# Attention followed by a two-level mixture of experts: earlier query loads, a split first load, regrouped gates, rare cases out of line

## The chip, the core and the metric

The kernel runs on one core of a Trainium2 chip. The metric is the device time of one execution in microseconds (us); before the change it is 521.31 us, the median of 3 runs (520.46 to 521.45). The profile that is read below is one further execution of the same kernel, with a span of 519.0 us.

The engines are named as the profile names them: PE is TensorE (matmuls), PEld its weight loads, DVE is VectorE, ACT is ScalarE, POOL is GpSimd, SP is SyncE, which here only starts transfers. A trailing q (ACTq, SPq) is the engine's instruction queue: waits, branches, register loads and the starting of transfers.

## The reference

Eight batches of attention with 16 query heads and one shared key/value head, then a mixture of experts in which a token goes to one group of four and to one expert of four in that group.

```python
# q: (8,16,384,64)   k, v: (8,1,384,64)   w1: (4,4,1024,1024)   w2: (4,4,1024,1024), all float32
scores = (q @ k^T) / 8
attn   = softmax(scores)                 # minus the row maximum, over 384 keys
x      = (attn @ v), heads joined        # (3072, 1024)
g_idx  = argmax(x @ w_group);  g_w = softmax(x @ w_group)[g_idx]
e_idx  = argmax(x @ w_expert[g_idx]);  e_w = softmax(...)[e_idx]
out    = g_w * e_w * (relu(x @ w1[g_idx, e_idx]) @ w2[g_idx, e_idx])
```

## The kernel before

**Tiling.** A batch's 16 heads times 384 queries are cut into six chunks of 2 x 512 query columns; two chunks make a *pair* `p`, so a batch has three pairs (`r` = 0, 1, 2) and the whole has 24. For every chunk `g` and each of three key tiles `kt`, `scores(g, kt)` (line 187) makes 128 x 1024 scores in one of two PSUM tiles `s` and ACT exponentiates them into `pt` (line 193). No row maximum is taken off. `values(g)` (line 247) multiplies `pt` by the values into the PSUM tile `o`, of which there is one. DVE sums the three exponent tiles (`pre_add`), and the column sums come either from a PE matmul (`sum_keys`, line 221, PSUM `kss`, turned by DVE into `krow`) or from a DVE transpose and reduction (`fold_keys`). `invert` (line 232) brings the sums to a PSUM tile `sm`, DVE takes the reciprocal `rc` and spreads it to `rinv`; `weigh` (line 256) multiplies `o` by it into `xT`, the layer's input for that batch, of which there is one buffer.

**Experts.** For each batch the gate has three steps: `gate_a` (line 269, PE: the sixteen-plus-four logits in partial sums `gps`, copied by ACT to `part`), `gate_b` (line 279, PE: `lps`; then `gate_math` on DVE and ACT), and `gate_c` (line 317, PE: counts `cps`; then the most frequent expert is found on DVE and GpSimd starts the 4 MB of that expert's weights). The whole batch is pushed through that expert; tokens of another expert are dealt with at the end, and with the given inputs at most one such (batch, expert) pair is left. The expert's work is cut into 14 units per batch (8 of `hps`, line 351, and 6 of `yps`, line 360) and `fill(n)` emits n of them. ACT takes `hps` and `yps` out of PSUM and SP stores `y`.

**Order.** Nothing is scheduled by the compiler: each engine's instructions run in the order in which this Python program emits them. The loop over pairs (line 407) has two forms. For `p` below `MOE_AT` = 7 (the *attention pairs*) no expert work exists yet, the column sums come from `sum_keys`, and the gates stand at the end of a pair: `gate_a` and `gate_b` of batch `b - 1` at the end of the pair with `r` = 0 (so in pairs 3 and 6), `gate_c` at the end of the pair with `r` = 1 (pairs 4 and 7). From pair 7 on (the *mixed pairs*) `fill` puts expert units between the parts of attention, and `gate_b` is emitted in pieces between the matmuls of a unit. At pair 7 that is done for batch 1, for which pair 6 has already done it.

**Loads.** `load_q(p)` (line 73) brings a pair's 512 KB of queries in four transfers of 128-byte runs; the tile `qraw` has three buffers, and the last reader of a buffer is `stats_q` (line 159), an ACT pass that sums squares. Both stand at the very end of a pair: `stats_q(p)`, then `load_q(p + 3)`. `prep_q(p + 1)` (line 177) is a DVE transpose of `qraw` into `qT` near the head of pair `p`. The keys and values of the next batch are started on ACT's queue (`load_kv`, line 81) at the end of a pair with `r` = 0. All transfers from SP and ACT share eight completion semaphores; a transfer waits until the one eight places before it has landed.

**Head and tail.** The kernel begins with 30 + 12 matmuls on ones (`warm`, lines 100 and 386), which compute nothing, while SP starts the first keys and then the first queries. At the end one more expert is applied to up to 128 collected tokens and scattered to the output (line 640); then every engine loads three flags into registers (lines 642 to 644), runs a loop over further (batch, expert) leftovers, here zero times (line 650), and a branch around a full recomputation for inputs whose scores are too large for the exponential without a maximum, here not taken (line 654).

Of the kernel before, what the change touches and what calls it, by code (L numbers as in the profile page):

```python
# [21 lines left out]
def kernel(  # L22
# [50 lines left out]
    def load_q(p):  # L73
        b, r = divmod(p, NCH // 2)
        t = pool.tile([P, NBP, 32], FP32, tag="qraw", bufs=3, name="qraw")
        for a in range(2):
            for j in range(2):
                nc.sync.dma_start(out=t[64 * a + 32 * j:64 * a + 32 * j + 32], in_=qv[b, a, j, :, r * NBP:(r + 1) * NBP])  # L78
        q_raw[p] = t

    def load_kv(b):
        kt = pool.tile([P, NB, 32], FP32, tag="k", name="k")
        for a in range(2):
            for j in range(2):
                (nc.sync if b == 0 else nc.scalar).dma_start(out=kt[64 * a + 32 * j:64 * a + 32 * j + 32], in_=kv[b, 0, j])
        k_raw[b] = kt
        vt = pool.tile([P, ST, D], FP32, tag="v", name="v")
        nc.scalar.dma_start(out=vt[:], in_=v[b, 0].rearrange("(st p) d -> p st d", st=ST))
        v_sb[b] = vt
# [12 lines left out]
    make_identity(nc, ident)  # L102
    load_kv(0)
    load_q(0)
# [164 lines left out]
    def gate_a(b):  # L269
        ps = ps_o.tile([P, CW], FP32, tag="o", name="gps")  # L270
        for r in range(2):
            for j in range(4):
                ko = 4 * r + j
                nc.tensor.matmul(out=ps[32 * j:32 * j + 32, 0:S], lhsT=gw[:, ko, :], rhs=xT[b][:, ko * S:(ko + 1) * S], start=(r == 0), stop=(r == 1), tile_position=(0, 32 * j))  # L274
        t = pool.tile([P, S], FP32, tag="part", bufs=1, name="part")
        nc.scalar.copy(out=t[:], in_=ps[:, 0:S])
        part[b] = t

    def gate_b(b, between=False):
        ps = (ps_m if between else ps_o).tile([P, ST, 32], FP32, tag="mm" if between else "o", name="lps")  # L280

        def logits(st):
            nc.tensor.matmul(out=ps[:, st, :], lhsT=part[b][:, st * P:(st + 1) * P], rhs=sel[:], start=True, stop=True)  # L283
        if between:
            for st in range(ST):
                inserts.append((0, lambda st=st: logits(st)))
            inserts.append((0, lambda: gate_math(b, ps)))
        else:
            for st in range(ST):
                logits(st)  # L290
            gate_math(b, ps)
# [25 lines left out]
    def gate_c(b):  # L317
        ps = ps_o.tile([P, ST, GE], FP32, tag="o", name="cps")
# [66 lines left out]
    for _ in range(12):  # L385
# [21 lines left out]
    for p in range(NP + 1):  # L407
# [3 lines left out]
        if p < NP:  # L411
            scores(g, 0)
            scores(g, 1)
            pre_add(g, 1)
# [6 lines left out]
        if p > 0:  # L421
            values(g - 2)
            if p - 1 < MOE_AT:
                sum_keys(p - 1)
# [3 lines left out]
        if p < NP:  # L428
            scores(g, 2)
            scores(g + 1, 0)  # L430
        if p > 0:
            if not busy:
                values(g - 1)
# [26 lines left out]
        if not busy:  # L460
            if r == 2 and b + 1 < B:
                stats_k(b + 1)
            if r == 0 and 0 < b < B:
                gate_a(b - 1)
                gate_b(b - 1)
            if r == 1 and b > 0:
                gate_c(b - 1)
            fold_last()
        elif p < NP:
# [7 lines left out]
            if r == 0 and 0 < b < B:  # L477
# [5 lines left out]
        if p < NP:  # L483
            stats_q(p)
            if p + 3 < NP:
                load_q(p + 3)
# [134 lines left out]
    nc.vector.tensor_copy(out=oki[:], in_=okf[:])  # L621

# [19 lines left out]
    ok = nc.values_load(oki[0:1, 0:1], min_val=0, max_val=1, skip_runtime_bounds_check_because="the result of a comparison")  # L642
    n_done = nc.values_load(nex[0:1, 0:1], min_val=0, max_val=1, skip_runtime_bounds_check_because="the result of a comparison")
    n_extra = nc.values_load(nex[0:1, 1:2], min_val=0, max_val=NPAIR, skip_runtime_bounds_check_because="a sum of 128 flags")

# [4 lines left out]
    with tc.For_i(n_done, n_extra, 1) as i:  # L650
# [3 lines left out]
    with tc.If(ok < 1):  # L654
        x_dram = nc.dram_tensor("x_t", [B * H, D, S], FP32).ap()
        qf = q.rearrange("b h (st p) d -> (b h) p st d", st=ST)
        kf = k.rearrange("b o (st p) d -> (b o) p st d", st=ST)
        vf = v.rearrange("b o (st p) d -> (b o) p st d", st=ST)
        with tc.For_i(0, B * H, 1) as i:
            bk = nc.s_assert_within(i >> 4, 0, B - 1, skip_runtime_bounds_check_because="the bits of an index below 128")  # L660
            qs = pool.tile([P, 4, ST, D], FP32, tag="qraw", bufs=3, name="qs")
            nc.sync.dma_start(out=qs[:, 0], in_=qf[bass.ds(i, 1)].rearrange("a p st d -> (a p) st d"))
            nc.sync.dma_start(out=qs[:, 1], in_=kf[bass.ds(bk, 1)].rearrange("a p st d -> (a p) st d"))
            vs = pool.tile([P, ST, D], FP32, tag="v", name="vs")
            nc.sync.dma_start(out=vs[:], in_=vf[bass.ds(bk, 1)].rearrange("a p st d -> (a p) st d"))
            qk = pool.tile([D, 2, S], FP32, tag="pt", bufs=8, name="qk")
            for a in range(2):
                tp = ps_m.tile([P, CW], FP32, tag="mm", name="tp")
                for st in range(ST):
                    nc.tensor.transpose(out=tp[0:D, st * P:(st + 1) * P], in_=qs[:, a, st, :], identity=ident[:])  # L670
                nc.vector.tensor_copy(out=qk[:, a, :], in_=tp[0:D, 0:S])
            ot = pool.tile([D, S], FP32, tag="rinv", bufs=1, name="ot")
            for qt in range(ST):
                sp = ps_s.tile([P, 2, CW], FP32, tag="s", name="sp")
                nc.tensor.matmul(out=sp[:, 0, 0:S], lhsT=qk[:, 0, qt * P:(qt + 1) * P], rhs=qk[:, 1, :], start=True, stop=True)
                sm1 = pool.tile([P, 4], FP32, tag="sm1", bufs=2, name="sm1")
                nc.vector.reduce_max(out=sm1[:, 0:1], in_=sp[:, 0, 0:S], axis=AX)
                nc.vector.tensor_scalar(out=sm1[:, 1:2], in0=sm1[:, 0:1], scalar1=-scale, scalar2=None, op0=OP.mult)
                at = pool.tile([P, S], FP32, tag="presum", bufs=3, name="at")
                nc.scalar.activation(out=at[:], in_=sp[:, 0, 0:S], func=ACTF.Exp, bias=sm1[:, 1:2], scale=scale)  # L680
                nc.vector.reduce_sum(out=sm1[:, 2:3], in_=at[:], axis=AX)
                nc.vector.reciprocal(out=sm1[:, 3:4], in_=sm1[:, 2:3])
                nc.vector.tensor_scalar(out=at[:], in0=at[:], scalar1=sm1[:, 3:4], scalar2=None, op0=OP.mult)
                tp = ps_m.tile([P, CW], FP32, tag="mm", name="tp")
                for kt in range(ST):
                    nc.tensor.transpose(out=tp[:, kt * P:(kt + 1) * P], in_=at[:, kt * P:(kt + 1) * P], identity=ident[:])
                av = pool.tile([P, S], FP32, tag="pt", bufs=8, name="av")
                nc.vector.tensor_copy(out=av[:], in_=tp[:, 0:S])
                op = ps_o.tile([P, CW], FP32, tag="o", name="op")
                for kt in range(ST):  # L690
                    nc.tensor.matmul(out=op[0:D, 0:P], lhsT=vs[:, kt, :], rhs=av[:, kt * P:(kt + 1) * P], start=(kt == 0), stop=(kt == ST - 1))
                nc.vector.tensor_copy(out=ot[:, qt * P:(qt + 1) * P], in_=op[0:D, 0:P])
            nc.sync.dma_start(out=x_dram[bass.ds(i, 1)].rearrange("a d s -> (a d) s"), in_=ot[:])
        xr = x_dram.rearrange("(b a hp) d s -> b a d hp s", b=B, a=2)
        zero = pool.tile([P, Dm], FP32, tag="pt", bufs=8, name="zero")
        nc.vector.memset(zero[:], 0.0)
        for b in range(B):
            xT[b] = pool.tile([P, KO * S], FP32, tag="xT", bufs=1, name="xT")
            for a in range(2):
                nc.sync.dma_start(out=xT[b][a * D:(a + 1) * D].rearrange("p (hp s) -> p hp s", hp=KO), in_=xr[b, a])  # L700
            xg = pool.tile([P, KO * S], BF16, tag="xbf", bufs=4, name="xg")
            nc.vector.tensor_copy(out=xg[:], in_=xT[b][:])
            nc.sync.dma_start(out=xb_dram[b], in_=xg[:])
            gate_a(b)
            gate_b(b)
            for st in range(ST):
                nc.sync.dma_start(out=outv[b, :, st, :], in_=zero[:])
        with tc.For_i(0, NPAIR, 1) as i:
            add_pair(i)
# [31 lines left out]
```

## Time and profile before

| | us |
|---|---|
| time, median of 3 | 521.31 |
| span of the profiled execution | 519.0 |
| start of the first scores matmul | 9.53 |
| starts of pairs 2, 3, 4, 5, 6, 7, 8 (first scores matmul) | 30.66, 43.99, 61.04, 75.22, 88.40, 105.51, 126.72 |
| end of the last ACT instruction (`yc`) | 508.7 |
| scatter started by GpSimd | 509.0 |

The starts of the pairs come from the timeline, which lists instructions in order of time, merged when alike and adjacent: start, duration, engine, line, operation, output and inputs, shapes, count, and in square brackets the idle time of the engine before it with what ended that idle time. The view of waits lists, for each engine and line, whom it waited for: total us, how often, the longest. PE's own waits are few, since it is busy nearly throughout, so the list of them is short and can be read as a whole.

### The profile page before, as it was taken

To read this page: it belongs to the slowest core of one execution; us is meant where nothing else is said; L and a number is where in the kernel's file an instruction comes from. 1 tells how busy PE (TensorE), PEld (TensorE's weight loads), DVE (VectorE), ACT (ScalarE), POOL (GpSimd) and SP (SyncE) were. 2 spreads that over 40 slices of the span, in tenths; PEclk is the share of its full clock that TensorE was granted. 3 is DMA by queue.
4 is the path that set the end of the run, shared out by engine and by line. 5 is a ranking of instruction groups with operands and counts; after the bars stand their busy time and mean duration, and the time that the engine had idled before them with its cause. 6 is when DMAs were issued, how large, how long until landed. Compare 5 with 4: busy or idle time off the path is not lost.

```text
span 519.0 us, 6961 instructions
## 1 busy us (share of the span) xinstructions
PE 487.0 (94%) x2605; PEld 205.8 (40%) x2605; DVE 342.8 (66%) x485; ACT 240.4 (46%) x342; POOL 63.7 (12%) x64
## 2 busy tenths in 40 slices
PE   6999889989999999999999999999989999998991
PEld 4233323334433444344433444344433444454550
DVE  3687577769948798779945995969856984322000
ACT  2645374426453645545635545454644742322331
POOL 1011113102101011101100030101110210210000
PEclk8999999999999999999999999999999999999996
DMA  9472249961995379754986299646963296699980
GB/s 127 45 83 42 72 63 177 208 134 15 201 201 178 60 122 216 175 119 78 212 136 199 48 170 204 180 79 118 214 110 127 56 201 130 185 232 248 226 224 14
DMA packets 148377, 73.06 MB, mean 141 GB/s; under 512 B 122587, under 2 KB 122587, under 8 KB 148336
## 3 DMA queue, kind: packets, MB, share of 16 engines
q0 software_dynamic: 19008, 37.84, 40.3%
q1 hardware_dynamic: 114928, 32.53, 30.2%
q10 hardware_dynamic: 14400, 2.16, 2.3%
q8 instruction: 23, 0.38, 0.3%
q14 instruction: 18, 0.15, 0.1%
HBM read 91.31 MB, written 19.40 MB: 213 GB/s over the span
## 4 chain that ended last, share of the span: by engine, by line
PE 61%; DMA 17%; SPq 7%; ACT 5%; DVE 5%; issue 3%; ACTq 1%; POOL 0%; POOLq 0%; DVEq 0%
PE s L191 17%; DMA qraw<-in_q_dram 14%; PE o L254 14%; PE yps L360 13%; PE hps L351 12%; SPq L78 7%; PE gps L274 2%; ACT pt L193 2%; DMA out_dram<-y 2%; DVE qT L182 2%; ACT junk L161 1%; PE kss L226 1%; ACT y L362 1%; DMA k<-in_k_dram 1%; PE lps L283 1%
## 5 line engine op out<-in xcount | busy, mean ns | idle before, releaser
L193 ACT ACTIVATE pt<-s 128x1024 f32<-128x1024 f32 x144 | 139.4, 1019 | 123.2 <-PE s L191 123.2
L191 PE MATMUL s<-qT,kT 64*128 64x512 f32 x576 | 145.1, 622 | 5.3 <-DVE qT L182 3.5
L254 PE MATMUL o<-pt,v 128*64 128x512 f32 x576 | 130.4, 598 | 0.0
L360 PE MATMUL yps<-w,hT 128*128 128x512 bf16 x384 | 90.0, 379 | 5.4 <-DVE rc L240 4.2
L351 PE MATMUL hps<-xbf,w 128*128 128x384 bf16 x512 | 89.2, 326 | 2.3 <-ACT hT L353 0.9
L201 DVE TENSOR_TENSOR presum<-pt 128x1024 f32<-128x1024 f32 x48 | 61.1, 1272 | 37.0 <-ACT pt L193 37.0
L263 POOL CAST xbf<-xT 128x1024 bf16<-128x1024 f32 x24 | 40.7, 1696 | 341.2 <-DVE xT L262 341.2
L191 PEld LDWEIGHTS s<-qT,kT 64*128 64x128 f32 x576 | 49.6, 188 | 64.8 <-issue 43.4
L254 PEld LDWEIGHTS o<-pt,v 128*64 128x64 f32 x576 | 38.6, 136 | 87.8 <-issue 74.9
L351 PEld LDWEIGHTS <-w 128*128 128x128 bf16 x512 | 48.7, 99 | 44.1 <-issue 14.5
L205 DVE TENSOR_TENSOR presum<-presum,pt 128x1024 f32<-128x1024 f32 x48 | 58.6, 1220 | 2.7 <-ACT hT L353 0.5
L362 ACT ACTIVATE y<-yps,gsel 128x512 f32<-128x512 f32 x48 | 32.9, 686 | 59.2 <-PE yps L360 55.2
L360 PEld LDWEIGHTS <-hT 128*128 128x128 bf16 x384 | 37.1, 101 | 56.7 <-issue 19.4
L182 DVE STREAM_TRANSPOSE qT<-qraw 128x1024 f32<-128x1024 f32 (+1 forms) x25 | 29.8, 1196 | 30.9 <-DMA qraw<-in_q_dram 24.8
L353 ACT ACTIVATE hT<-hps 128x384 bf16<-128x384 f32 x64 | 31.2, 490 | 39.6 <-PE hps L351 37.1
L213 DVE STREAM_TRANSPOSE turn<-presum 128x1024 f32<-128x1024 f32 x34 | 42.4, 1246 | 1.2
L217 DVE TENSOR_REDUCE fold<-turn 128x32 f32<-128x1024 f32 x34 | 41.5, 1220 | 1.2
L161 ACT ACTIVATE junk<-qraw 128x1024 bf16<-128x1024 f32 x24 | 25.2, 1052 | 15.3 <-DMA k<-in_k_dram 15.2
L242 DVE STREAM_TRANSPOSE rinv<-rc 128x1024 f32<-128x1024 f32 x24 | 29.9, 1245 | 0.8
L262 DVE TENSOR_TENSOR xT<-o,rinv 128x1024 f32<-128x1024 f32 x24 | 29.4, 1225 | 1.3
L240 DVE RECIPROCAL rc<-sm 128x32 f32<-128x32 f32 x24 | 8.0, 335 | 24.7 <-PE sm L236 15.4
L93 POOL DMA_DIRECT2D w<-in_moe_w_dram x18 | 12.6, 704 | 61.0 <-DVE gsel L339 42.4
(130 smaller groups left out, 179.9 us busy)
## 6 DMA issues: line engine op xcount, KB each, us to landing
w<-in_moe_w_dram POOLq DMA_DIRECT2D x18, 1024.0 KB, 13.4
w<-in_moe_w_dram POOLq DMA_DIRECT2D x9, 2048.0 KB, 24.3
qraw<-in_q_dram SPq DMA_DIRECT2D x96, 128.0 KB, 3.8
out_dram<-y SPq DMA_DIRECT2D x48, 256.0 KB, 3.7
x_bf<-xbf SPq DMA_DIRECT2D x8, 768.0 KB, 3.3
k<-in_k_dram ACTq DMA_DIRECT2D x28, 48.0 KB, 2.3
v<-in_v_dram ACTq DMA_DIRECT2D x8, 96.0 KB, 2.6
xe<-x_bf SPq DMA_DIRECT2D x1, 768.0 KB, 9.7
```

The source lines that it names most:

```text
L182: nc.vector.transpose(out=t[:, i * w:(i + 1) * w], in_=src[:, i * w:(i + 1) * w])
L191: nc.tensor.matmul(out=ps[:, par, :], lhsT=kT[b][r, kt * P:(kt + 1) * P], rhs=qT[g][r, :], start=True, stop=True)
L193: nc.scalar.activation(out=t[:], in_=ps[:], func=ACTF.Exp, scale=scale)
L201: nc.vector.tensor_add(out=t[:], in0=pt[g, 0][:], in1=pt[g, 1][:])
L205: nc.vector.tensor_add(out=t[:], in0=t[:], in1=pt[g, 2][:])
L213: nc.vector.transpose(out=t[:], in_=presum[g][:].rearrange("p a n -> p (a n)"))
L217: nc.vector.reduce_sum(out=fold[p][:, ch, :], in_=t[:].rearrange("p (b i) -> p b i", i=32), axis=AX)
L254: nc.tensor.matmul(out=o_ps[p][64 * par:64 * par + 64, ch, :], lhsT=v_sb[b][:, kt, :], rhs=pt[g, kt][:, par, :], start=(kt == 0), stop=(kt ...
L263: nc.gpsimd.tensor_copy(out=xbf[b][:, cs], in_=xT[b][:, cs])
L351: nc.tensor.matmul(out=ps[:, 0:S], lhsT=w1[:, ko, fc * P:(fc + 1) * P], rhs=xb[:, ko * S:(ko + 1) * S], start=(ko == 0), stop=(ko == KO - 1))
L360: nc.tensor.matmul(out=ps[:], lhsT=state["h"][:, fo, st * P:(st + 1) * P], rhs=w2[:, fo, nh * CW:(nh + 1) * CW], start=(fo == 0), stop=(fo ...
L362: nc.scalar.activation(out=y, in_=ps[:], func=ACTF.Copy, scale=gs[:, st:st + 1])
```

## The change

The change has five parts.

1. **Query loads at the head.** `stats_q(p)` and `load_q(p + 3)` move from the end of pair `p` to just after its first two `scores`.
2. **First loads over two queues.** The first query tile is loaded in two halves by SP, ahead of everything else; the first keys go to ACT's queue and the first values to SP's. The second group of warm-up matmuls grows from 12 to 36. `values(0)` is emitted in pair 0 instead of pair 1.
3. **First gates over two pairs.** For batches 0 and 1, `gate_a` moves from the end of pairs 3 and 6 to just after the first two `scores` of pairs 4 and 7; `gate_b` of batch 0 to the middle of pair 4, before `values`; batch 1 keeps only the `gate_b` of pair 7; `gate_c` of batch 0 moves behind `fold_last`. These use the PSUM pair `mm` in place of the single tile `o`. The last batch's `gate_b` uses `mm` too.
4. **`sum_keys`** of the attention pairs moves from before to after the middle two `scores`.
5. **Rare cases out of line.** One flag, "anything rare to do", is worked out from the two existing ones and loaded into a register of every engine before the last expert units; the loop and the recomputation, with their own register loads, stand inside one branch that is placed out of line.

```diff
-    def load_q(p):
+    def load_q(p, parts=1):
...
-                nc.sync.dma_start(out=t[64 * a + 32 * j:64 * a + 32 * j + 32], in_=qv[b, a, j, :, r * NBP:(r + 1) * NBP])
+        n = NBP // parts
+        for i in range(parts):
...
-                (nc.sync if b == 0 else nc.scalar).dma_start(out=kt[64 * a + 32 * j:64 * a + 32 * j + 32], in_=kv[b, 0, j])
+                nc.scalar.dma_start(out=kt[64 * a + 32 * j:64 * a + 32 * j + 32], in_=kv[b, 0, j])
-        nc.scalar.dma_start(out=vt[:], in_=v[b, 0].rearrange("(st p) d -> p st d", st=ST))
+        (nc.sync if b == 0 else nc.scalar).dma_start(out=vt[:], in_=v[b, 0].rearrange("(st p) d -> p st d", st=ST))
...
+    load_q(0, 2)
     load_kv(0)
-    load_q(0)
...
     prep_k(0)
-    for _ in range(12):
+    for _ in range(36):
         nc.tensor.matmul(out=warm[:, 0:P], lhsT=ones_bf[:], rhs=ones_bf[:], start=True, stop=True)
...
             scores(g, 0)
             scores(g, 1)
+            stats_q(p)
+            if p + 3 < NP:
+                load_q(p + 3)
+            if r == 1 and 1 < p <= MOE_AT:
+                gate_a(b - 1, True)
             pre_add(g, 1)
...
-            values(g - 2)
-            if p - 1 < MOE_AT:
+            if p > 1:
+                values(g - 2)
+            if busy and p - 1 < MOE_AT:
                 sum_keys(p - 1)
...
             scores(g + 1, 0)
+        if p == 0:
+            values(0)
         if p > 0:
             if not busy:
+                sum_keys(p - 1)
+                if r == 1 and 0 < b < B:
+                    gate_b(b - 1)
                 values(g - 1)
                 invert(p - 1)
...
-            if r == 0 and 0 < b < B:
-                gate_a(b - 1)
-                gate_b(b - 1)
+            fold_last()
             if r == 1 and b > 0:
-                gate_c(b - 1)
-            fold_last()
+                gate_c(b - 1, True)
...
-            if r == 0 and 0 < b < B:
+            if r == 0 and MOE_AT <= p - r and 0 < b < B:
                 gate_a(b - 1)
...
-        if p < NP:
-            stats_q(p)
-            if p + 3 < NP:
-                load_q(p + 3)
...
+    nc.vector.tensor_tensor(out=raref[:, 0:1], in0=small[0:1, 1:2], in1=small[0:1, 0:1], op=OP.is_gt)
+    nc.vector.tensor_scalar(out=raref[:, 1:2], in0=okf[:], scalar1=-1.0, scalar2=1.0, op0=OP.mult, op1=OP.add)
+    nc.vector.tensor_add(out=raref[:, 0:1], in0=raref[:, 0:1], in1=raref[:, 1:2])
...
+    nc.vector.tensor_copy(out=rarei[:], in_=raref[:, 0:1])
+    rare = nc.values_load(rarei[0:1, 0:1], min_val=0, max_val=2, skip_runtime_bounds_check_because="a sum of two comparisons")
...
-    with tc.For_i(n_done, n_extra, 1) as i:
+    rare_block = tc.If(rare > 0, preferred_fallthrough_block=False)
+    with rare_block:
...
+      with tc.For_i(n_done, n_extra, 1) as i:
         add_pair(pair_of(ids[0:1, bass.ds(i, 1)]))
```

## The prediction

> **What bounds the kernel now.** I read the page's busy line first, then PE's own waits, then the timeline where those waits lie. PE is busy 94% of the span; no other engine is above 66%:
>
> ```profile
> PE 487.0 (94%) x2605; PEld 205.8 (40%) x2605; DVE 342.8 (66%) x485; ACT 240.4 (46%) x342; POOL 63.7 (12%) x64
> ```
>
> So the time is PE's work plus its gaps. The gaps are 519.0 - 487.0 = 32 us: about 1.4 before the first matmul, 11 after the last (PE's last matmuls end at 508), and some 20 in PE's waits, the largest of which are:
>
> ```profile
> PE yps L360 <- DVE rc L240: 4.2, 4, 1.6
> PE s L191 <- DVE qT L182: 3.5, 1, 3.5
> PE sm L236 <- DVE krow L228: 1.4, 1, 1.4
> PE lps L283 <- ACT part L276: 1.2, 2, 0.6
> PE gps L274 <- DVE xT L262: 1.2, 1, 1.2
> PE cps L319 <- DVE xT L262: 1.2, 1, 1.2
> PE gps L274 <- issue: 1.1, 1, 1.1
> ```
>
> The reader should see three families: the head (`s` waits for `qT`), the gates in the attention pairs (`gps`, `lps`, `cps`, `sm`), and four waits in the mixed pairs. The timeline around one of these four shows its cause:
>
> ```profile
> 267.29 1.25 DVE L182 STREAM_TRANSPOSE qT<-qraw 128x1024 f32<-128x1024 f32 x1 [6.07 <-DMA qraw<-in_q_dram]
> ...
> 268.46 0.32 DVE L240 RECIPROCAL rc<-sm 128x32 f32<-128x32 f32 x1
> 268.82 1.25 DVE L242 STREAM_TRANSPOSE rinv<-rc 128x1024 f32<-128x1024 f32 x1
> 268.83 1.45 PE L360 MATMUL yps<-w,hT 128*128 128x512 bf16 x6 [1.20 <-DVE rc L240]
> ```
>
> Queries land late, DVE waits 6.07 us for them, `rc` stands behind that transpose on DVE, and the PSUM buffer that `rc` must read is the one the next `yps` needs. At the end, the branch around the recomputation (line 654) is what the span waits for:
>
> ```profile
> L654 PEldq COMPARE_BRANCH  x1: 3762/3762/3762, 514.2 to 514.2; - x1
> ```
>
> PE takes 3.76 us for it, after the scatter has landed (SP and ACT leave line 650's waits at 513.4).
>
> [...] the granted clock is 0.50 from about 9.45 to 12.9, 3.4 us, after PE stood idle from 6.01 to 9.53. Before 9.45 the record shows 1.00, but the 30 first warm-up matmuls took 3.38 us, 0.113 each, against 0.061 for the same size in line 632 (32 in 1.95), so I take that stretch as half rate too. [...] each start takes 0.4 to 0.6 us on SP, and from 9 to 11 us the DMA engines have work throughout. [...]
>
> **Part 2, the head.** Now: keys are started at 1.03 to 2.49, the four query transfers at 3.00 to 4.79, landed at 8.74; two transposes; `s` at 9.53, and at half clock. After: four half-size query transfers (2048 packets of 128 B) start at 1.03 on SP beside the keys (1536) on ACT's queue. The first 6 us moved 4168 packets on SP's queue in the 3.95 us from 2.05, 1055 per us; 3584 packets need 3.4 us, so both are there at 5.5, and with 0.58 for `kT` and 0.67 for half a `qT` the scores could start at 6.7. But 66 warm-up matmuls stand ahead of them: 42 end at 6.1 as now, and if the clock rises there [...], the other 24 take 1.5: 7.6. All at half rate would give 1.35 + 66 x 0.113 = 8.8[...]. I take **7.6**, at full clock. Pairs 0 and 1 hold 12 score calls of 0.98, two `values` of 2.73, `kss` 1.5, `sm` 0.36: 19.1. I add 2.5 of gaps: ACT paces the six calls of pair 0 (0.97 each, plus 1.06 for `stats_q`, now in their midst), and ACT's 2.4 us of starting the next keys and values, hidden under `values(0)` and `kss` today, now has only two score calls beside it. Pair 2 starts at 29.2 instead of 30.66: **1.4 saved**[...].
>
> **Part 3, the gates.** An attention pair without a gate takes 13.2 to 13.3 (75.22 to 88.40; 30.66 to 43.99), all PE work. Pairs 3 and 4 take 31.2 (43.99 to 75.22). After, they hold two plain pairs, 26.5, plus `gate_a` 1.53, `lps` 0.8, `cps` 0.2: 29.0, since `gate_a` finds `xT` finished a pair ago, `part` has `values` and `kss` to be copied beside, and `cps` has its own PSUM: **2.2 saved**. The wait added is DVE's: `gate_math` (2.2 us) now stands ahead of `rc` in pair 4. Its `ex` needs ACT, which by then is through with the middle exponents, and PE has 2.73 of `values` to do meanwhile, so I cost it at nothing. Pairs 6 and 7 take 38.3 (88.40 to 126.72). Pair 6 becomes plain, 13.3, and its gate of batch 1 (`gps`, `lps` and `gate_math`, a part of it repeated in pair 7) is gone; pair 7 stays 21.2, plus `gate_a` 1.53, less the 1.4 wait for `krow`: 34.6, **3.7 saved**. That wait ended late because ACT worked off `stats_q` ahead of the pair's first exponents, and DVE's transpose queued behind those.
>
> **Part 4** costs nothing: DVE turns `kss` in 0.68 while PE does 2.73 of `values`.
>
> **Part 1, queries in the mixed pairs.** The late transfers are those started at the end of an `r` = 1 pair, just as 4 MB of weights start (126.7): SP's queue stalls 10.95 us over them at 130.13. A pair earlier, they are 18 us ahead of the weights; the transfers that collide then are those of the next pair, which have two whole pairs (37 us) against a longest landing of 25. All **4.2** of `yps <- rc` go. On ACT the 1.06 us pass lies in a gap of some 5 us ahead of the third exponent. Stores behind the stalled SP queue are placed as now.
>
> **Part 5, the tail.** Today from scatter landed (513.4) to the end is 5.6. After, PE is at its final branch at about 508, so the 3.76 lie beside the scatter; left are GpSimd's 0.40 and 1.05 (its semaphore write and drain, at 514.1 and 514.6) and the closing 1.0: 2.5. **3.1 saved.** Against it: PE's register load of the flag waits for DVE. `pq` ends at 480.33; `bd`, `bdp`, `okf` and `oki` end at 481.32, three more small operations in the chain at 0.15 to 0.2 each bring 482.0, the load takes 0.49 (as at line 642): 482.5 instead of 480.69, **1.8 lost** with all expert units behind it. It could be 0.5 less if part of it lies under queued matmuls. `lps` of the last batch takes a buffer of `yps`: 0.3 lost. Net 1.0.
>
> **Sum**: 1.4 + 2.2 + 3.7 + 4.2 + 1.0 = 12.5; 521.3 - 12.5 = **508.8 us**.
>
> **Rivals.** (a) Queries still come late, with the collision only moved by a pair, or SP's stall moves to the stores and ACT runs out of `y` buffers (today once, 2.5 us). For it: DMA engines are full during weights. Against: 37 us of slack. Then the 4.2 stay: 513.0. (b) The end is cheaper than I think: the flag's load hides, [...] and no gap opens in pair 1. 1.8 + 0.6 + 1.5 more: 504.9. (c) Slower: the regrouping makes DVE late. It is busy 10 to 10.9 of 13.3 us in an attention pair, and pair 4 adds 4 us to it; if `sm` waits 2 us in each of pairs 1 to 6 (12 us), the 5.9 of the gates are not won and the mixed pairs keep their 4.2, it is 521.3 - 1.4 - 1.0 + 12 = 530.9. Against it: `krow` was late by only 1.4, once.
>
> **Chances.** Forecast 0.72, (a) 0.14, (b) 0.10, (c) 0.04. Bounds of the forecast: head +1.2/-0.6, gates and queries +1.5/-0.5, tail +1/-1. The range reaches towards (a) and (b): 505.5 to 513.0. Faster 0.95, same 0.01 (part of (c) met half-way), slower 0.04.
>
> **What would show it.** PE's waits should no longer have `yps <- rc`, nor `gps`, `lps` or `cps` in pairs 3 to 7; first `s` near 7.6 with no clock of 0.50 after it; pair 8 starting near 119.4, 7.3 earlier than now; DVE's waits for `qraw` gone but for the first; a new PE gap of 1.8 before a `hps` some 36 us before the end; no branch of 3.8 after the scatter. A DVE wait for `krow` or queries in the mixed pairs, or a late landing of the scatter, would prove me wrong.

## The result, and the profile after

The changed kernel takes **509.41 us** (median of 4, 509.16 to 509.46) against 521.09 for the kernel before beside it: a ratio of 0.9776, 95% interval 0.9759 to 0.9793. The forecast was 508.8. The span of the profiled execution fell from 519.0 to 507.9, by 11.1 us. The sum came out close, but in part by luck: one term missed by 6.0 us, and the others together came out 4.7 us better than forecast.

Busy time of the kernel after, from its page. PE has 4 us less to do and 7 us fewer gaps (507.9 - 482.7 = 25.2 against 32):

```profile
PE 482.7 (95%) x2603; PEld 205.1 (40%) x2623; DVE 345.0 (68%) x480; ACT 241.6 (48%) x341; POOL 63.7 (13%) x64
```

PE's own waits in the kernel after (total us, how often, the longest):

```profile
PE sm L238 <- DVE krow L230: 4.4, 1, 4.4
PE s L193 <- ACT pt L195: 3.4, 9, 1.3
PE hps L353 <- DVE rarei L633: 2.0, 1, 2.0
PE warm L102 <- DVE ones_bf L98: 1.3, 1, 1.3
PE yps L362 <- ACT y L364: 1.3, 4, 0.4
PE s L193 <- DVE qT L184: 0.9, 1, 0.9
```

`yps <- rc` (4.2 in four waits) is gone, and so are `gps`, `cps` and `lps <- part`. The wait for the flag (`rarei`) is the one forecast. The first line was not: `krow`, 1.4 before and forecast to vanish, is now the largest wait of all, and it lies in pair 7.

Pair 15 in the kernel after, from the timeline; this is the place that showed a wait of 1.20 before. The transpose of the queries (line 184) no longer waits, `rc` follows `sm`, and `yps` starts without a wait:

```profile
255.39 1.24 DVE L184 STREAM_TRANSPOSE qT<-qraw 128x1024 f32<-128x1024 f32 x1
258.22 0.26 PE L240 MATMUL sm<-fold,sel 128*64 128x32 f32 x4
258.53 0.36 DVE L242 RECIPROCAL rc<-sm 128x32 f32<-128x32 f32 x1 [1.90 <-PE sm L240]
260.33 1.04 PE L362 MATMUL yps<-w,hT 128*128 128x512 bf16 x3
```

The branch at the end, from the view of line 660 of the kernel after. It still takes 3.8 us on PE, but PE is there before GpSimd starts the scatter (500.79), so it lies beside the transfer. From the scatter's start to the end it is now 7.1 us; before it was 10.0.

```profile
L660 PEldq COMPARE_BRANCH  x2: 95/1957/3819, 497.1 to 500.1; - x2
```

Where the 11.1 us came from, by stretches of PE's timeline (in the last two rows, of DVE's and GpSimd's):

| stretch | before | after | saved | forecast |
|---|---|---|---|---|
| to the start of pair 2 | 30.66 | 28.18 | 2.5 | 1.4 |
| pair 2 | 13.33 | 12.79 | 0.5 | 0 |
| pairs 3 and 4 | 31.23 | 27.84 | 3.4 | 2.2 |
| pair 5 | 13.18 | 12.90 | 0.3 | 0 |
| pairs 6 and 7 | 38.32 | 40.65 | -2.3 | 3.7 |
| pair 8 to the bound check (`sq`, line 615) | 352.33 | 347.46 | 4.9 | 4.2 - 0.3 |
| bound check to the scatter's start | 29.95 | 30.97 | -1.0 | -1.8 |
| scatter's start to the end | 10.0 | 7.1 | 2.9 | 3.1 |
| sum | 519.0 | 507.9 | 11.1 | 12.5 |

### The profile page after: what moved, and what is told of

It reads as the page before. It is cut to its first block, busy times and chain, and to the rows that moved or that the text cites. A ratio compares the mean times of both kernels' runs of the same rounds, so it can differ in the third digit from the quotient of the medians.

```text
span 507.9 us, 6898 instructions
## 1 busy us (share of the span) xinstructions
PE 482.7 (95%) x2603; PEld 205.1 (40%) x2623; DVE 345.0 (68%) x480; ACT 241.6 (48%) x341; POOL 63.7 (13%) x64
## 3 DMA queue, kind: packets, MB, share of 16 engines
q10 hardware_dynamic: 15600, 2.26, 2.6%
## 5 line engine op out<-in xcount | busy, mean ns | idle before, releaser
L203 DVE TENSOR_TENSOR presum<-pt 128x1024 f32<-128x1024 f32 x48 | 63.6, 1325 | 46.9 <-ACT pt L195 46.9
L362 PE MATMUL yps<-w,hT 128*128 128x512 bf16 x365 | 86.8, 379 | 2.6 <-ACT y L364 1.3
L95 POOL DMA_DIRECT2D w<-in_moe_w_dram x18 | 12.5, 704 | 66.1 <-DVE gsel L341 45.9
## 6 DMA issues: line engine op xcount, KB each, us to landing
w<-in_moe_w_dram POOLq DMA_DIRECT2D x9, 2048.0 KB, 23.7
```

The costliest lines, as they stand in the source:

```text
L203: nc.vector.tensor_add(out=t[:], in0=pt[g, 0][:], in1=pt[g, 1][:])
L362: nc.tensor.matmul(out=ps[:], lhsT=state["h"][:, fo, st * P:(st + 1) * P], rhs=w2[:, fo, nh * CW:(nh + 1) * CW], start=(fo == 0), stop=(fo ...
```

## The experiments

Theory: each part of the change does what its row says, and the row that failed, pairs 6 and 7, failed because ScalarE is held up there while it starts the keys of batch 3. Rivals: VectorE is overloaded in pair 7, or transfers can't be started at all while the weights are being loaded. The first four runs below are about that; the run with the gates back asks what brought it on, and the others price one part each. Three groups of four kernels ran, each beside the kernel before (520.4, 520.8 and 520.9 us).

### What holds pair 7 up

PE's timeline in pair 7 of the kernel after:

```profile
101.62 2.79 PE L256 MATMUL o<-pt,v 128*64 128x512 f32 x12
108.78 0.62 PE L238 MATMUL sm<-krow,selq 128*64 128x16 f32 x8 [4.36 <-DVE krow L230]
109.33 3.79 PE L193 MATMUL s<-qT,kT 64*128 64x512 f32 x8
```

The wait is only the first half of the damage: the eight score matmuls behind it take 3.79 us, where 1.99 is usual. The answer by windows (PE, PEld, DVE, ACT, POOL busy with counts, then the granted clock, DMA share, GB/s) shows why: while PE waits the granted clock falls to 0.50 (at 106.74 by the clock record), and by the share of 0.61 in the last line it stays there until about 113.6, 4.8 us after PE has work again.

```profile
104.00:108.00 4.00, 0.41 (x2) 0.00 (x0) 2.35 (x3) 3.02 (x5) 0.00 (x0) 0.84 0.47 143
108.00:110.00 2.00, 1.22 (x10) 1.04 (x12) 1.16 (x4) 0.00 (x0) 0.00 (x0) 0.50 1.18 168
110.00:112.00 2.00, 2.00 (x6) 0.68 (x4) 1.90 (x2) 0.55 (x1) 0.00 (x0) 0.50 0.52 74
112.00:114.00 2.00, 2.00 (x11) 0.96 (x8) 0.40 (x1) 1.32 (x2) 1.04 (x1) 0.61 0.00 0
```

Following the wait back: DVE turned `krow` at 107.96, because it stood 5.96 us, until 105.65, for the exponents `pt`; ACT's queue in the same stretch:

```profile
94.28 0.32 ACTq L87 DMA_DIRECT2D k<-in_k_dram  x1
94.34 1.02 ACT L195 ACTIVATE pt<-s 128x1024 f32<-128x1024 f32 x1
94.64 7.25 ACTq L87 DMA_DIRECT2D k<-in_k_dram  x3
103.25 0.39 ACTq L90 DMA_DIRECT2D v<-in_v_dram  x1
103.68 1.94 ACT L195 ACTIVATE pt<-s 128x1024 f32<-128x1024 f32 x2 [8.32 <-DMA k<-in_k_dram]
```

The exponents of pair 7 stand 8.32 us behind the starts of batch 3's keys and values. The third line joins three starts; taken singly, two take 0.5 each from 94.64, and the last begins only at 101.57. What it waits for can be worked out. In the trace the transfers from SP and ACT have eight completion semaphores among them, numbers 100, 102 and 104 to 109, and from pair 9's queries on they are taken in turn: the four query transfers have 104 to 107, the first three key transfers 108, 100 and 102 (109 went to the store of `xbf`), the fourth again 104, as the first of the query transfers, and the values 105, as the second. Those were started by SP at 85.96 and 86.32, in the middle of the weights (started at 76.0), and the view of `qraw` gives their times to landing:

```profile
DMA to landing us min/median/max: 15.6/16.9/16.9
```

85.96 + 15.6 = 101.6 and 86.32 + 16.9 = 103.2: the two times at which ACT goes on. The semaphores in the trace say the same: the fourth key start waits for number 104, which the first of those query transfers raised at 101.55 (ACT goes on at 101.57), and the start of the values for number 105, which the second raised at 103.22 (103.25).

**Keys and values of batch 3 at the head of pair 6.**

```diff
+            if p == 6:
+                load_kv(3)
             stats_q(p)
             if p + 3 < NP:
                 load_q(p + 3)
...
-        if r == 0 and b + 1 < B:
+        if r == 0 and b + 1 < B and p != 6:
             load_kv(b + 1)
```

> The changed kernel, with one load moved: the keys and values of batch 3 are started (on ScalarE, as before) at the head of pair 6, ahead of that pair's query load, and no longer at the end of pair 6, behind it. Theory (shared completion slots): in the changed kernel PE's 4.4 us wait for krow in pair 7 comes from ScalarE, which stands from 94.6 to 101.9 at the start of these loads because they take over completion semaphores of the query load of pair 9, which is itself stuck behind 4 MB of weights; started first, they find their slots free, the five starts take 2.2 to 2.6 us as in the kernel before, krow's wait falls to under 0.5, the eight scores behind it take 2.0 instead of 3.8, and pair 7 takes 21.6 instead of 27.9: 503.1 us. Rival (the transfer engines are full from 76 to 103, and whoever starts a load in that time stands): ScalarE stands for 7 us in pair 6 instead, 509.4 or more. Rival (krow is late because VectorE is overloaded): no change, 509.4.

Measured: 506.52 us (ratio 0.9733, 0.9711 to 0.9754), faster than the changed kernel by half of what was expected. `krow`'s wait is gone, but a wait of 2.5 us of PE for `pt` has come in pair 6. ACT's timeline there:

```profile
84.25 2.30 ACTq L87 DMA_DIRECT2D k<-in_k_dram  x3
92.24 0.39 ACTq L90 DMA_DIRECT2D v<-in_v_dram  x1
92.76 1.06 ACT L163 ACTIVATE junk<-qraw 128x1024 bf16<-128x1024 f32 x1 [7.78 <-PE sm L238]
```

The four key starts went through in 2.7 us while weights were being loaded, though the keys took 9.0 to 17.0 us to land (median over the keys in the kernel after: 2.5); that speaks against the second rival. The start of the values stood until PE had finished with the values of pair 5 (92.03): a batch's values have two buffers, and until then both are in use. So the edit put another wait in, and isn't a clean test.

**The keys alone at the head of pair 6,** the values at its end as before (`load_kv` split into `load_k` and `load_v`):

```diff
+            if p == 6:
+                load_k(3)
             stats_q(p)
...
-        if r == 0 and b + 1 < B:
+        if p == 6:
+            load_v(3)
+        elif r == 0 and b + 1 < B:
             load_kv(b + 1)
```

> As the run with batch 3's keys and values moved to the head of pair 6, but only the keys; the values stay at the end of pair 6. In that run the four key starts took 2.6 us in the middle of the weights, and only the start of the values stood, 5.7 us, until PE's values of pair 5, the last readers of their buffer, had ended (92.03; started at 92.24). Theory (shared completion slots): keys now find free slots, the values take over a slot of pair 8's queries, landed long before, and their buffer is free at the end of pair 6; neither stands, krow's 4.4 us wait is gone, pair 7 takes 21 to 21.6 us: 502.5 to 503.5 us. Rival (a start stands whenever the engines are full of weights): the values' start stands up to 7 us at the end of pair 6, and the time stays at 506.5 or more.

Measured: **502.29 us** (0.9649, 0.9628 to 0.9670). ACT's starts of keys and values:

```profile
84.22 2.23 ACTq L87 DMA_DIRECT2D k<-in_k_dram  x3
94.33 0.39 ACTq L92 DMA_DIRECT2D v<-in_v_dram  x1
```

Both lie in the middle of the weights (8.9 to 18.0 us to landing for the keys, 10.0 for the values), neither stands, `krow` isn't among PE's waits, and from pair 7's reciprocal on the kernel is 4.7 us ahead of the changed one at first and 6.8 from pair 9 on. Only the place of four starts was changed, ahead of pair 9's queries instead of behind them; no load was taken out. Together with the semaphores above that shows the cause: the slots, not the load on VectorE and not the transfer engines.

**Keys and values of later batches on SyncE.**

```diff
-                nc.scalar.dma_start(out=kt[...], in_=kv[b, 0, j])
+                (nc.scalar if b == 0 else nc.sync).dma_start(out=kt[...], in_=kv[b, 0, j])
...
-        (nc.sync if b == 0 else nc.scalar).dma_start(out=vt[:], ...)
+        nc.sync.dma_start(out=vt[:], ...)
```

> The changed kernel, with all keys and values of batches 1 to 7 started on SyncE's queue instead of ScalarE's, at the same places. Theory: what cost time is that ScalarE's exponents stood behind the start of a load; SyncE has nothing urgent in these pairs, so the 6.3 us of pair 7 go as in the run with the early load, and 1.0 us of the 1.3 in pair 1 (exponents behind the start of batch 1's keys): 502.1 us. Rival: SyncE's queue, which already stands 14 us behind the weights, gets longer, and keys, queries or stores of y come late in the mixed pairs: ScalarE waits for y buffers or VectorE for k, 505 to 509 us.

Measured: **502.21 us** (0.9639, 0.9614 to 0.9664). The waits for `krow` and the 1.3 us of `s` for `pt` in pair 1 are both gone; pairs 6 and 7 take 33.8 us (80.77 to 114.59). SyncE now starts batch 3's keys at 100.85, which is soon enough, since they are wanted in pair 8. This kernel serves as the base for pricing the parts in the middle, because its attention pairs have no such stall.

**Gates at their old places** (part 3 undone: `gate_a`, `gate_b`, `gate_c` and their PSUM buffers as in the kernel before), once with the keys on ScalarE and once with them on SyncE.

```diff
-            if r == 1 and 1 < p <= MOE_AT:
-                gate_a(b - 1, True)
...
-                if r == 1 and 0 < b < B:
-                    gate_b(b - 1)
...
-            fold_last()
+            if r == 0 and 0 < b < B:
+                gate_a(b - 1)
+                gate_b(b - 1)
             if r == 1 and b > 0:
-                gate_c(b - 1, True)
+                gate_c(b - 1)
+            fold_last()
```

> The changed kernel with part 3 undone: first gates at their old places and PSUM buffers (a gate's projection and logits at the end of pairs 3 and 6, its counts ahead of the last presums in pairs 4 and 7). Theory (part 3 moved the start of batch 3's keys into the window of the weights): the end of pair 6 comes about 27 us after the start of the first weights instead of 18, the weights take about 26, so the keys are started freely and krow's 4.4 us go; pairs 3 and 4 lose 2.4 (31.2 before, less 1.0 from the moved kss, against 27.8 now), pairs 6 and 7 gain 3.4 (37.3 against 40.7): 508.4 us, so that part 3 as a whole was worth nothing. Rival (the stall comes from the order of query and key loads alone, part 1): it stays, and part 3 was worth its 2.4 plus some 1 to 3 in pairs 6 and 7: 512 to 515 us.

> Keys and values on SyncE's queue (502.2 us), and the gates back at their old places: what part 3 is worth once the stall of pair 7 is out of the way. Theory (my sum for part 3 was right but for the stall): pairs 3 and 4 lose 2.4, pairs 6 and 7 lose 37.3 - 33.8 = 3.5 (37.3: before, less 0.5 for each moved kss; 33.8: the sync run), together 5.9: 508.1 us, no better than the gates undone with keys on ScalarE (507.7). Rival (part 3 was worth little in itself, the waits only moved): 503 to 504 us.

Measured: 507.67 us (0.9753, 0.9732 to 0.9773) on ScalarE, 506.61 (0.9735, 0.9711 to 0.9759) on SyncE. In the first, batch 3's keys are started at 101.60, in 1.88 us, since pair 6 with its gate ends that much later and the last of the weights have landed (at 99.5, an estimate: in the kernel after they are started 2.1 us behind `gsel` and land 23.7 us later, and here `gsel` is at 73.69); `krow`'s wait is 0.9. So in the changed kernel part 3 made nothing faster: its profile reaches the last pair's reciprocal 1.1 us later than this one. Measured on the SyncE base, the same part is worth 4.5 us (reciprocals of pair 7 at 108.20 against 103.71, and 4.5 apart to the end): 2.2 of it in pairs 3 to 5, 2.3 in pairs 6 and 7. The 5.9 expected were too much mainly because they took in the old wait of 1.4 for `krow`, which this kernel doesn't have. **Part 3 set the stall off**: it took a gate out of pair 6 and so moved the start of the keys from behind the weights into the middle of them. But it needed part 1 as well, which had put pair 9's queries ahead of the keys: with the keys started first (the run with the keys alone) there is no stall, though they too start in the middle of the weights.

### What the other parts are worth

**Queries back at the end of a pair,** on the SyncE base (`stats_q` and `load_q` behind `load_kv`).

```diff
-            stats_q(p)
-            if p + 3 < NP:
-                load_q(p + 3)
...
             load_kv(b + 1)
+        if p < NP:
+            stats_q(p)
+            if p + 3 < NP:
+                load_q(p + 3)
```

> Keys and values on SyncE's queue (502.2 us), and the query loads with their ScalarE pass back at the end of a pair. Theory (part 1 is worth the four waits of yps for rc): the query loads of pairs 9, 15, 18 and 21 land behind the weights again, VectorE stands for qraw, yps waits about 1 us four times: 506.4 us, with 20 us or more of VectorE waits for qraw against 0.9. Rival (the other changes moved weights and queries apart anyway): under 1 us of such waits, 502.2 to 503.

Measured: 507.07 us (0.9745, 0.9715 to 0.9775). Waits of PE and of DVE in this kernel:

```profile
PE yps L362 <- DVE rc L242: 3.5, 4, 1.1
DVE qT L184 <- DMA qraw<-in_q_dram: 25.3, 7, 6.0
```

The four waits are back, with VectorE's 25 us for queries behind them. In the reciprocals the kernel loses 1.5 us up to pair 7 and 4.1 from there to the end. The first I had not priced: 0.6 is lost by pair 1, and 0.9 in pair 7, where `krow` is waited for again (0.7) when ACT has its query pass ahead of the pair's first exponents.

**Key sums back ahead of the middle scores,** on the SyncE base.

```diff
-            if busy and p - 1 < MOE_AT:
+            if p - 1 < MOE_AT:
                 sum_keys(p - 1)
...
             if not busy:
-                sum_keys(p - 1)
```

> Keys and values on SyncE's queue (502.2 us), with the kss matmuls back ahead of the middle scores, as in the kernel before. Theory (part 4 isn't free as I had it: kss there takes 1.6 instead of 1.06 us in pairs 2 to 6, because its last half waits for VectorE's presum; behind two more score calls the presum is ready): 0.5 in five pairs, 504.7 us. Rival (my prediction's cost of nothing: the plain pair went from 13.3 to 12.8 for another reason, the query pass or load leaving the pair's end): 502.2 us.

Measured: 505.12 us (0.9693, 0.9665 to 0.9720). PE's timeline in pair 2, of this kernel first and then of the changed one:

```profile
32.20 1.60 PE L228 MATMUL kss<-presum,ones 128*32 128x512 f32 x8
```

```profile
34.80 1.06 PE L228 MATMUL kss<-presum,ones 128*32 128x512 f32 x8
```

Eight equal matmuls take 0.54 longer, because the last four wait for `presum`. The reciprocals of pair 1 to pair 7 lose 2.5 us, five times 0.5. Such a wait hides inside a group of instructions: PE's list of waits doesn't have it. The view of line 226 of the kernel before does, among the waits of its matmuls and weight loads (`presum`, 4.0 us in seven waits).

**The warm-up at 12, and the first loads as before.**

```diff
-    for _ in range(36):
+    for _ in range(12):
```

> The changed kernel with 12 matmuls in the second warm-up loop instead of 36. PE then ends the warm-up at about 5.2 (30 in 3.26 from 1.34, 12 at 0.060) and stands some 2.3 us until the queries are there; the first scores start at 7.5 as now, since the data and not the warm-up set them. Theory (an idle gap loses the clock: 4.4 us idle in pair 7 and, in two runs, 2.0 us idle ahead of the last units were followed by some 3.4 us of halved clock): the first scores run at half rate, 2.0 to 3.8 us for eight, and pair 2 starts 1 to 1.7 later: 510.4 to 511.1 us. Rival (2.3 us is short enough, as in most runs ahead of the last units): 509.4, same stage times as the changed kernel. My prediction took the warm-up as what sets the first scores; then 12 would start them earlier than 7.5.

Measured: 511.16 us (0.9818, 0.9789 to 0.9847), whose interval overlaps the changed kernel's (up to 0.9793). The profiled execution shows no change: scores at 7.55 and at full rate, all stages up to the scatter within 0.4 us of the changed kernel's, and its own time is 508.56; the other three took 510.4 to 512.0. PE stood 1.54 us ahead of the first scores, not the 2.3 expected. **Inconclusive**: the mean is slower, and the mean granted clock of the other three is lower (0.986 to 0.988 against 0.991), which would fit a stretch at a lower clock, but that was not shown: no profile of such an execution exists.

```diff
-    load_q(0, 2)
     load_kv(0)
+    load_q(0)
...
-                nc.scalar.dma_start(out=kt[...], in_=kv[b, 0, j])
+                (nc.sync if b == 0 else nc.scalar).dma_start(out=kt[...], in_=kv[b, 0, j])
```

> The changed kernel, but with batch 0's keys and the first queries loaded as in the kernel before: keys first on SyncE, then the queries in four whole transfers behind them, values on ScalarE; warm-up of 36 kept. Theory (the first scores wait for data): first scores at 9.5 as before, 2.0 later than now; PE idles 2.9 us behind the warm-up (until 6.6), so the clock may fall, which costs up to 1.7 more: 511.4 to 513.1 us. Rival (the longer warm-up alone bought the gain, by keeping the clock): scores late by less than 1 us, 509.4 to 510.4.

Measured: 512.23 us (0.9834, 0.9809 to 0.9859). First scores at 9.58, no clock lost at the head (granted 1.00 from 5 to 16), and every later stage up to the scatter 2.1 to 2.4 us late. The time of landing sets the first scores; the long warm-up alone doesn't bring them forward. PE's timeline at the head of the changed kernel says the same, with a wait for data of 0.90 behind the last warm-up matmul:

```profile
1.34 3.26 PE L102 MATMUL warm<-ones_bf 128*128 128x128 bf16 x30 [1.34 <-DVE ones_bf L98]
4.44 2.17 PE L388 MATMUL warm<-ones_bf 128*128 128x128 bf16 x36
7.51 1.99 PE L193 MATMUL s<-qT,kT 64*128 64x512 f32 x8 [0.90 <-DVE qT L184]
```

**The tail undone, and the flag loaded late.** The first takes part 5 back; the second keeps it and moves one line.

```diff
-    rare = nc.values_load(rarei[0:1, 0:1], ...)
     while begun[0] < B or units:
         fill(1)
...
+    rare = nc.values_load(rarei[0:1, 0:1], ...)
     rare_block = tc.If(rare > 0, ...)
```

> The changed kernel with part 5 undone: no flag, no register load ahead of the last units, three register loads and the two rare blocks in line at the end, as in the kernel before. Theory A (as predicted: the tail saves 2.9 behind the scatter, and the wait for the flag costs its whole 1.8 to 2.0): 509.4 + 1.0 = 510.4 us. Theory B (the flag's wait is mostly covered, because the second expert weights of the last, compacted pair land at 495.5 in any case: the run with the flag late won 0.5, and there py waited 0.8 for w): 509.4 + 2.9 - 0.5 = 511.8 us, with a wait of py for w and the branch of 3.8 us after the scatter.

> The changed kernel, with the register load of the flag for the rare cases moved from ahead of the last expert units to just ahead of the branch, behind the scatter. Theory: PE no longer waits for rarei ahead of hps (2.0 us), and the load lies behind PE's last matmul, where 0.5 us of it beside the scatter costs at most 0.5: 507.4 to 507.9 us. Rival (PE's work was only shifted and the tail is set by something else, such as the stores of y): 509.4. Rival (load and branch now end after the scatter's landing): 0.5 to 1 of the 2.0 is lost again, 508.2.

Measured: 511.24 us (0.9809, 0.9780 to 0.9838) without part 5, and 508.58 (0.9771, 0.9747 to 0.9794) with the flag late; the second is 0.7 slower than the theory had it and can't be told from the changed kernel by its time alone. From the last pair's reciprocal, the kernel without part 5 has its scatter 70.95 us later and ends at 80.8; the changed one 72.15 and 79.2; with the flag late 71.47 and 78.4. So part 5 saves 2.8 behind the scatter and loses 1.2 ahead of it, net 1.6, between the two theories. Why 1.2 and not 2.0 is shown by PE's waits from the last units on, in the kernel without part 5 and in the one with the late flag. Both have a wait that the changed kernel doesn't have:

```profile
PE py L643 <- DMA w<-in_moe_w_dram: 0.3, 1, 0.3
```

```profile
PE py L650 <- DMA w<-in_moe_w_dram: 0.8, 1, 0.8
```

The second weights of the compacted pair are started when the batch before lets go of their buffer (469.2 with the flag late) and land 26.5 us later; an earlier PE meets them. Both kernels also wait 0.4 for `hT` just there, which the wait for the flag covers. 2.0 less 0.3 and 0.4 is 1.3 against the 1.2 measured; 2.0 less 0.8 and 0.4 is 0.8 against 0.7.

**Both together**: keys on SyncE and the flag late.

> Keys and values on SyncE's queue and the flag's register load just ahead of the branch. Theory (both gains stand side by side; the profile of the run with keys on SyncE had lost 2.0 us to the flag and 1.7 to the halved clock after it, of which the landing of the last weights gives back some): 502.2 less 0.5 to 2.4: 499.8 to 501.7 us. Rival (the last weights, which start when the batch before lets go of their buffer, land no earlier and take all of it): 502.2.

Measured: **500.49 us** (500.19 to 500.56; 0.9607, 0.9582 to 0.9631), faster than the kernel before and the changed one, and within what was expected. Its interval overlaps that of keys on SyncE alone (0.9614 to 0.9664). Its busy line, from the page, with 17 us of gaps:

```profile
PE 481.7 (97%) x2603; PEld 205.8 (41%) x2623; DVE 345.2 (69%) x480; ACT 241.5 (48%) x341; POOL 63.8 (13%) x64
```

## Why the prediction was right, and where it was wrong

**Head: right time, wrong reason, so luck.** First scores at 7.51 against 7.6, but the step "the warm-up stands ahead of them" failed: data set the time. ACT's wait for the keys ended at 6.25, where the forecast had them at 5.5; `kT` ran from 6.29, and half a `qT` from 6.79 to 7.46. The clock, taken to rise at 6.1 as before (first clock record, full, at 6.05), has its first record, full, at 4.34 in the kernel after, and the second loop took only 2.17 us and was over at 6.6. Pair 2 came 1.0 earlier than forecast: pairs 0 and 1 took 18.6 us of work and 2.1 of gaps, not 19.1 and 2.5. The work had `kss` at 1.5, and in pair 1 it takes 1.06.

**Gates: the sum was right, its neighbour was not looked at.** Pairs 3 and 4 saved 3.4, of which 1.0 belongs to part 4. For pairs 6 and 7 the forecast had 34.6; without the stall they take 33.8, and 34.3 in the run that also takes part 4 back (which moved `kss` in pair 6 but not in pair 7). The failed step is "less the 1.4 wait for `krow`": I explained that wait by the query pass on ACT alone, took it as gone, and did not ask where ACT's own transfer starts would fall once pair 6 was shorter and pair 9's queries were started ahead of them. In place of no wait there were 4.4 us, so one of the prediction's own signs of being wrong came up. The cost was 6.8: 4.4 of waiting, 1.8 of slow scores, and the rest in the units behind them. Rival (c) named this wait, as an overloaded VectorE; the run with early keys shows that VectorE was the messenger. ACT's timeline in pair 7 of the kernel before had the evidence: even the query pass stood behind the starts of those keys.

```profile
109.35 1.06 ACT L161 ACTIVATE junk<-qraw 128x1024 bf16<-128x1024 f32 x1 [2.59 <-DMA k<-in_k_dram]
```

**Part 4: "costs nothing" was wrong by 2.5 us in our favour.** I priced DVE's turn of `kss` and not the wait of `kss` for `presum`. PE's timeline of the kernel before held the evidence: 1.61 for the eight matmuls of line 226 in pairs 2 and 6, 1.06 in pair 1.

**Queries: right.** 4.2 forecast; 4.1 measured by undoing it on the SyncE base, and 1.5 more up to pair 7, which I had not priced.

**Tail: right in kind, 0.6 better in size.** 3.1 became 2.9, the 0.3 for the last `lps` is there (40.86 to 41.18 us from the last reciprocal to the bound check), and the term of 1.8 for the flag, a wait of 2.0, cost 1.0 to 1.2 net, because it covers shorter waits behind it. The branch did not become cheap: PE took 3762 ns for it before and 3819 ns after. It only became parallel.

**Summary.** 12.5 forecast, 11.1 in the profile and 11.7 in the medians. Short by 6.0 in pairs 6 and 7; over by 1.1 in the head, 2.0 in pairs 2 to 5, 1.0 from pair 8 to the bound check, and 0.6 in the tail. That these nearly cancel is luck, and it hid a stall whose removal was worth 7 us (509.41 to 502.29 with the early keys). Past pair 8, undoing part 1 brings back 4.1, with the four waits at 3.5 and not 4.2; the 1.0 gained beyond the forecast stays open.

## What to carry to other kernels

When a change shortens a stretch, list what every queue *starts* at the end of that stretch, and ask what will be in flight at the new time: here removing a gate moved an innocent key load into the weights and cost more than the gate. Here ScalarE, a compute engine that also starts transfers, stood 8.32 us at starts whose completion slots were still taken by transfers of another queue, so it is worth trying the starts on a queue with nothing urgent behind them (502.21 us against 509.41). And a group of equal instructions that takes longer in one place than in another is worth a look whatever the list of waits says: here it was a hidden wait (`kss`, 1.60 us against 1.06) or a halved clock (the scores of pair 7, 3.79 against 1.99).

## What the runs showed of the hardware

- **Behind 2.0 us of idle PE, matmuls ran slower in three of ten profiles.** Ten profiles have the same 2.0 us wait for the flag; in three of them (keys on SyncE, the same with the key sums back, keys and values of batch 3 first) the 56 matmuls after it took 10.94 us, in the other seven 9.26. PE's timeline with keys on SyncE, and with the early keys:

```profile
465.37 10.94 PE L353 MATMUL hps<-xbf,w 128*128 128x384 bf16 x56 [2.02 <-DVEq L660]
```

```profile
466.36 9.26 PE L359 MATMUL hps<-xbf,w 128*128 128x384 bf16 x56 [2.02 <-DVEq L670]
```

  In the first the granted clock is 0.50 from 467 to 469; by the shares around that (0.81 from 465 to 467, 0.84 from 469 to 471) it fell at 466.24 and rose at 469.64, 3.40 later.

  The times at which the granted clock changes lie whole multiples of 3.413 us apart in the clock records of the kernels before and after: before 6.05, 9.47, 12.88 and 511.23 (1, 1 and 146 of them), after 4.34, 106.74, 113.57 and 502.69 (30, 2 and 114). If such steps also run on between the changes, which is an estimate from these times, the wait with keys on SyncE (463.35 to 465.37) lies inside the one step that ends with the fall (462.83 to 466.24), and in the kernel after, which kept the clock, an edge at 471.97 falls inside the wait (471.11 to 473.13). A step idle for 59% would then have lost the clock, and one idle for 34% not; that this decides it was not shown beyond these two.
- **The same warm-up does not always take the same time.** The 36 matmuls of its second loop took 2.17, 2.26, 3.29 and 3.51 us in four profiles (the kernel after, key sums back on SyncE, first loads as before, both edits together); in the last of these the warm-up and not the data set the first scores (7.96).
- **Starting a transfer took long on one queue, while starts on another went through.** In pair 6 of the kernel after, SP stood 10.76 us in the start of one 128 KB query transfer, from 86.93 to 97.69, with a DMA share of 1.20 to 1.23 in that stretch. In the same stretch, from 94.28 on, ACT made three starts of 48 KB of keys in 0.32, 0.48 and 0.48 us. Landing was slow on both queues (15.6 to 16.9 us for the queries started from 85.96 on, against a median of 3.8; 7.6 to 7.7 for those keys, against a median of 2.5), but the time to start was not shared. Whether the queue itself makes the difference, or the size of the transfers and what already stood in the queue, no run here separates.
